# Chunked attention ahead of an expert router: the attention of a tile spread over six iterations, row sums taken from a ones column

## The chip, the cores and the metric

The kernel runs on one core of a Trainium2 chip. The metric is the device time of one execution in microseconds (us). Engines are named as in the profile: PE is TensorE, with PEld its weight loads; DVE is VectorE; ACT is ScalarE; POOL is GpSimd; SP is SyncE, here only a queue that issues DMA transfers.

## What is computed

Two blocks follow each other. The first is attention inside chunks of 64 rows, the second a router that sends each row to one of eight experts.

```
q, k, v: (B=8, H=8, S=576, Dh=64), fp32;  N = B*S = 4608, D = H*Dh = 512
for each batch, head and chunk of 64 rows:
    scores = (q k^T) / 8;  a = exp(scores - rowmax);  a /= rowsum(a) + 1e-9
    out = a v
x = out as (4608, 512)
logits = (x/|x|) (emb/|emb|)^T / tau            # 8 experts
expert = argmax(logits);  gate = softmax(logits)[expert]
y = gate * (relu(x w1[expert]) w2[expert])      # w1 (8,512,1024), w2 (8,1024,512)
```

## The kernel before

The order of instructions on every engine is the order in which the program text issues them; each engine works through its own queue in that order and waits on semaphores where data or a buffer is not ready.

**Attention.** The 4608 rows are 36 tiles of 128 rows; a tile holds two chunks of each of eight heads, which are four pairs. `load_qk` fetches a q and a k tile (256 KB each, in pieces of 256 bytes, split in two where a tile straddles two batches) through SP's queue; `load_v` fetches a whole batch of v as eight transfers, one for each head. For a tile t:

- `turn_qk` transposes k and q on PE (four 128x128 transposes each) and copies kT by ACT and qT by DVE from PSUM to SBUF.
- `scores` makes 16 products of 64x64 (each shows as two instructions in the profile), takes the row maximum and subtracts it on DVE, applies exp on ACT, and sums the rows on DVE (the line `nc.vector.tensor_reduce(rs, a, ...)`), adds 1e-9 and inverts.
- `turn_a` transposes the weights a and copies aT by ACT.
- `values` makes 16 products with v, multiplies by the inverted sums on DVE into x, writes x to DRAM through POOL's queue, and squares x on ACT with a running sum into `nsq`.
- `turn_x` transposes x and copies xT by DVE; `logits` multiplies it with the normalised expert embeddings into one PSUM bank that holds the logits of all tiles.

One iteration t of the loop issues, in this order: `turn_a(t)`, `turn_qk(t+1)`, `scores(t+1)`, `turn_x(t-1)`, `values(t)`, the loads for later tiles, and `logits(t-1)`. The output of `values` goes into the other half of the PSUM banks that held the tile's scores. Every fourth iteration `load_first` fetches one of eight 2 MB weight matrices (w1 and w2 of expert 0 and expert 7, and each a second time into the second slots).

[...] Before, the pool `ps_s` has two tiles of two banks, `ps_t` (all transposes) three of one, `ps_l` one.

**Seam.** A chain of small DVE operations and 36 products sorts the rows by expert into 40 blocks.

**Experts.** For each of the 40 blocks rows are gathered, transposed, multiplied by w1, passed through relu, transposed, multiplied by w2, scaled and scattered. The weights lie in two slots on each of two sides; a block whose expert's weights are not yet in its slot loads them.

The functions around the change:

## Time and profile before

| | |
|---|---|
| median of 3 runs | 1045.79 us (1044.2 to 1046.27) |
| profiled execution, its own time | 1047.4 us |
| span of the profiled execution | 1045.6 us |
| PE busy in the span | 907.6 us (87%) |
| DVE busy | 268.5 us (26%) |
| ACT busy | 173.1 us (17%) |
| POOL busy | 103.9 us (10%) |
[...]

Times in the rows are microseconds from the span's start. Busy time is the time in which an engine has an instruction in work. Matmuls overlap each other, so the distance between two starts says more than a duration. [...]

### The profile page before, as it was taken

To read this page: it belongs to the slowest core of one execution; us is meant where nothing else is said; L and a number is where in the kernel's file an instruction comes from. 1 tells how busy PE (TensorE), PEld (TensorE's weight loads), DVE (VectorE), ACT (ScalarE), POOL (GpSimd) and SP (SyncE) were. 2 spreads that over 40 slices of the span, in tenths; PEclk is the share of its full clock that TensorE was granted. 3 is DMA by queue.
4 is the path that set the end of the run, shared out by engine and by line. 5 is a ranking of instruction groups with operands and counts; after the bars stand their busy time and mean duration, and the time that the engine had idled before them with its cause. 6 is when DMAs were issued, how large, how long until landed. Compare 5 with 4: busy or idle time off the path is not lost.

```text
span 1045.6 us, 15287 instructions
## 1 busy us (share of the span) xinstructions
PE 907.6 (87%) x6287; PEld 485.3 (46%) x6287; DVE 268.5 (26%) x508; ACT 173.1 (17%) x310; POOL 103.9 (10%) x128
## 2 busy tenths in 40 slices
PE   4777777767777745899999999999999999999998
PEld 4666666656666635333333333333333333333332
DVE  3444444343444466111111111111111111111110
ACT  3222222222222220011111011011111101101111
POOL 0000000000000000101111101101110110111101
PEclk9855555555555555899999999999999999999999
DMA  8555465457374100101013575167942142316670
GB/s 204 147 150 168 113 185 171 116 162 200 88 207 133 40 21 1 51 19 41 21 41 121 202 261 202 41 226 285 345 162 106 51 186 106 121 41 233 229 256 2
DMA packets 153670, 142.58 MB, mean 136 GB/s; under 512 B 115702, under 2 KB 115702, under 8 KB 153600
## 3 DMA queue, kind: packets, MB, share of 16 engines
q1 hardware_dynamic: 144256, 112.21, 34.6%
q0 software_dynamic: 9344, 29.39, 7.9%
q8 instruction: 50, 0.82, 0.3%
q14 instruction: 20, 0.16, 0.0%
HBM read 391.14 MB, written 19.92 MB: 393 GB/s over the span
## 4 chain that ended last, share of the span: by engine, by line
issue 56%; PE 21%; DVE 14%; POOL 5%; ACT 2%; POOLq 0%; DMA 0%; SPq 0%
PE lg_ps L226 6%; PE tr L136 6%; PE sc L154 4%; POOL xin L515 4%; PE tr L181 3%; DVE mx L162 2%; DVE a L164 2%; DVE qT L141 2%; DVE rs L172 2%; ACT a L170 2%; DVE xT L220 2%; POOL out_dram L583 2%; PE inv L451 1%; DVE rs L173 1%; DMA kx<-in_k_dram 0%
## 5 line engine op out<-in xcount | busy, mean ns | idle before, releaser
L541 PE MATMUL h_ps<-w,xbT 128*64 128x512 f32 x1280 | 284.5, 597 | 2.4 <-DVE xbT L531 2.4
L574 PE MATMUL y_ps<-w,hT 128*64 128x512 f32 x1280 | 283.3, 595 | 0.0
L541 PEld LDWEIGHTS h_ps<-w,xbT 128*64 128x64 f32 x1280 | 92.3, 138 | 186.5 <-issue 183.3
L574 PEld LDWEIGHTS y_ps<-w,hT 128*64 128x64 f32 x1280 | 88.5, 137 | 167.0 <-issue 167.0
L552 DVE TENSOR_SCALAR h<-h_ps 128x512 f32<-128x512 f32 x40 | 27.7, 692 | 377.9 <-PE h_ps L541 377.9
L226 PE MATMUL lg_ps<-enT,xT 128*128 128x8 f32 x288 | 64.2, 352 | 62.3 <-DVE xT L220 62.3
L583 POOL DMA_INDIRECT out_dram<-y,dst_row x40 | 40.6, 1014 | 532.6 <-ACT y L582 517.2
L226 PEld LDWEIGHTS lg_ps<-enT,xT 128*128 128x128 f32 x288 | 60.8, 312 | 69.2 <-DVE xT L220 69.1
L582 ACT ACTIVATE y<-y_ps,gate_at 128x512 f32<-128x512 f32 x40 | 27.5, 688 | 272.9 <-PE y_ps L574 272.9
L550 ACT ACTIVATE h<-h_ps 128x512 f32<-128x512 f32 x40 | 23.9, 598 | 285.1 <-PE h_ps L541 285.1
L154 PE MATMUL sc<-kT,qT 64*64 64x64 f32 x1152 | 40.7, 317 | 31.5 <-DVE qT L141 31.5
L566 DVE COPY hT<-ht_ps 128x512 f32<-128x512 f32 x40 | 27.7, 692 | 136.6 <-PE ht_ps L562 136.6
L141 DVE COPY qT<-tr 128x512 f32<-128x512 f32 x36 | 24.9, 691 | 136.5 <-PE tr L136 136.5
L154 PEld LDWEIGHTS sc<-kT,qT 64*64 64x64 f32 x1152 | 35.0, 218 | 44.9 <-issue 42.4
L209 POOL DMA_DIRECT2D x_rows<-x x36 | 19.6, 544 | 352.3 <-DVE x L202 352.3
L562 PEld LDWEIGHTS ht_ps<-ident,h 128*128 128x128 f32 x320 | 34.3, 140 | 32.5 <-issue 32.5
L515 POOL DMA_INDIRECT xin<-x_rows,src_row x40 | 41.0, 1024 | 49.5 <-DVE dst_row L465 37.6
L170 ACT ACTIVATE a<-a 128x512 f32<-128x512 f32 x36 | 22.7, 630 | 132.5 <-DVE a L164 132.5
L562 PE MATMUL ht_ps<-ident,h 128*128 128x128 f32 x320 | 43.7, 280 | 0.0
L194 PE MATMUL sc<-v,aT 64*64 64x64 f32 x1152 | 40.8, 318 | 0.0
L136 PE MATMUL tr<-ident,kx 128*128 128x128 f32 x144 | 36.4, 405 | 4.9 <-DMA kx<-in_k_dram 4.9
L218 PE MATMUL tr<-ident,x 128*128 128x128 f32 x144 | 40.0, 433 | 0.0
(118 smaller groups left out, 605.4 us busy)
## 6 DMA issues: line engine op xcount, KB each, us to landing
w<-in_moe_w_dram SPq DMA_DIRECT2D x168, 2048.0 KB
v<-in_v_dram SPq DMA_DIRECT2D x64, 144.0 KB
x_rows<-x POOLq DMA_DIRECT2D x36, 256.0 KB, 2.3
qx<-in_q_dram SPq DMA_DIRECT2D x32, 256.0 KB
kx<-in_k_dram SPq DMA_DIRECT2D x32, 256.0 KB
qx<-in_q_dram SPq DMA_DIRECT2D x8, 128.0 KB
kx<-in_k_dram SPq DMA_DIRECT2D x8, 128.0 KB
xin<-x_rows,src_row POOLq DMA_INDIRECT x40, 3.5
```

Source lines behind the costliest of these rows:

```text
L136: nc.tensor.transpose(ps[:, i], a[:, i * P : i * P + P], ident)
L141: nc.vector.tensor_copy(x, ps)
L154: nc.tensor.matmul(sc[CH * c : CH * c + CH, par, i], lhsT=qx[r0 : r0 + CH, i, c0 : c0 + CH], rhs=kx[r0 : r0 + CH, i, c0 : c0 + CH], start= ...
L170: nc.scalar.activation(a, a, AF.Exp, scale=scale)
L194: nc.tensor.matmul(pv[CH * c : CH * c + CH, par, i], lhsT=d["aT"][r0 : r0 + CH, i, CH * c : CH * c + CH], rhs=v_t[b][r0 : r0 + CH, i, cb], ...
L218: nc.tensor.transpose(ps[:, c], d["x"][:, c * P : c * P + P], ident)
L226: nc.tensor.matmul(lg_ps[:, t], lhsT=d["xT"][:, c], rhs=enT[:, c], start=(c == 0), stop=(c == KD - 1),)
L515: nc.gpsimd.indirect_dma_start(out=t, out_offset=None, in_=x_rows, in_offset=bass.IndirectOffsetOnAxis(ap=src_row[:, j : j + 1], axis=0), ...
L541: nc.tensor.matmul(ps[G * s : G * s + G], lhsT=d["xT"][:, c, G * s : G * s + G], rhs=w1_sb[s][j % 2][:, c, fh * 512 : fh * 512 + 512], sta ...
L562: nc.tensor.transpose(ps[:, c], d["h"][:, f0 : f0 + P], ident)
L574: nc.tensor.matmul(ps[G * s : G * s + G], lhsT=d["hT"][:, c, G * s : G * s + G], rhs=w2_sb[s][j % 2][:, c], start=(c == 0), stop=(c == KF ...
L583: ins = nc.gpsimd.indirect_dma_start(out=out, out_offset=bass.IndirectOffsetOnAxis(ap=dst_row[:, j : j + 1], axis=0), in_=y, in_offset=Non ...
```

## The change

An iteration t now issues: `turn_a(t)`, `turn_qk(t+3)` with the load of tile t+7 behind it, `logits(t-2)`, `scores(t+2)`, `turn_x(t-1)`, `values(t)` with loads of v, `weights(t+2)` (the exp alone), `norm(t)` (the square alone). The loop runs from -3 to 37. Each v tile has a column of ones behind the 64 columns of a head (in rows of 72), filled by POOL, so that the products of `values` have 65 columns, the last of which is the row sum; the sum on DVE is gone, and 1e-9 and the inversion follow the products. The products of `values` have two PSUM banks of their own, and the scores' pool has one tile of two banks instead of two such tiles. xT is copied by ACT instead of DVE. Of the eight weight loads four are issued together in iteration 12; the other four, for the second slots, are issued behind the attention's part, in a pool that is opened there.

```diff
-    w1_sb = [[keep.tile([P, KD, F], FP32, name=f"w1_{s}{i}") for i in range(2)] for s in range(2)]
+    w1_sb = [[keep.tile([P, KD, F], FP32, name=f"w1_{s}0")] for s in range(2)]
...
+    def load_first(i):
+        for s in range(2):
+            e = (0, E - 1)[s]
+            nc.sync.dma_start(out=w1_sb[s][i], in_=w1_rows[:, e * KD : e * KD + KD, :])
...
+    VW = 72
-        tc.tile_pool(name="qk", bufs=3) as qk_p,
+        tc.tile_pool(name="qk", bufs=4) as qk_p,
-        tc.tile_pool(name="ps_s", bufs=2, space=PSUM) as ps_s,
+        tc.tile_pool(name="ps_s", bufs=1, space=PSUM) as ps_s,
+        tc.tile_pool(name="ps_v", bufs=1, space=PSUM) as ps_v,
...
-            t = v_p.tile([P, NPAIR, NCB, Dh], FP32, tag="v", name="v")
+            t = v_p.tile([P, NPAIR, NCB, VW], FP32, tag="v", name="v")
+            nc.gpsimd.memset(t[:, :, :, Dh : Dh + 1], 1.0)
             for h in range(H):
                 r0 = CH * (h % 2)
                 nc.sync.dma_start(
-                    out=t[r0 : r0 + CH, h // 2],
+                    out=t[r0 : r0 + CH, h // 2, :, 0:Dh],
...
-            a = wk.tile([P, NPAIR, 2, CH], FP32, tag="a", name="a")
+            a = wk.tile([P, NPAIR, 2, CH], FP32, tag="a", name="a", bufs=3)
...
+            st[t] = {"a": a}
+
+        def weights(t):
+            a = st[t]["a"]
             nc.scalar.activation(a, a, AF.Exp, scale=scale)
-            rs = wk.tile([P, NPAIR, 2], FP32, tag="rs", name="rs")
-            nc.vector.tensor_reduce(rs, a, axis=AX.X, op=ALU.add)
-            nc.vector.tensor_scalar(rs, rs, 1e-9, None, ALU.add)
-            nc.vector.reciprocal(rs, rs)
-            st[t] = {"ps": ps, "a": a, "rs": rs}
...
-            pv = d["ps"][:, :, NPAIR * CH :].rearrange("p r (i d) -> p r i d", d=Dh)
+            ps = ps_v.tile([P, 2, 512], FP32, tag="pv", name="pv")
+            pv = ps[:, :, 0 : NPAIR * (Dh + 1)].rearrange("p r (i d) -> p r i d", d=Dh + 1)
...
-                            rhs=v_t[b][r0 : r0 + CH, i, cb],
+                            rhs=v_t[b][r0 : r0 + CH, i, cb, 0 : Dh + 1],
...
+            rs = wk.tile([P, 2, NPAIR], FP32, tag="rs", name="rs")
+            nc.vector.tensor_scalar(rs, pv[:, :, :, Dh], 1e-9, None, ALU.add)
+            nc.vector.reciprocal(rs, rs)
+            x = wk.tile([P, NPAIR, 2, Dh], FP32, tag="x", name="x", bufs=3)
             nc.vector.tensor_tensor(
                 x.rearrange("p i r d -> p r i d"),
-                pv,
-                d["rs"].rearrange("p i r -> p r i").unsqueeze(3).to_broadcast([P, 2, NPAIR, Dh]),
+                pv[:, :, :, 0:Dh],
+                rs.unsqueeze(3).to_broadcast([P, 2, NPAIR, Dh]),
...
+        def norm(t):
             junk = one.tile([P, D], FP32, tag="junk", name="junk")
-            nc.scalar.activation(junk, x, AF.Square, accum_out=nsq[:, t : t + 1])
+            nc.scalar.activation(junk, st[t]["x"], AF.Square, accum_out=nsq[:, t : t + 1])
...
-            nc.vector.tensor_copy(xT, ps)
+            nc.scalar.copy(xT, ps)
...
-        for t in range(NT + 1):
+        for t in range(-3, NT + 2):
+            if 0 <= t < NT:
                 turn_a(t)
-            if t + 1 < NT:
-                turn_qk(t + 1)
-                scores(t + 1)
-            if t > 0:
+            if t + 3 < NT:
+                turn_qk(t + 3)
+                if t + 7 < NT:
+                    load_qk(t + 7)
+            if 0 <= t - 2:
+                logits(t - 2)
+            if 0 <= t + 2 < NT:
+                scores(t + 2)
+            if 0 <= t - 1 < NT:
                 turn_x(t - 1)
-            if t < NT:
+            if 0 <= t < NT:
                 values(t)
-                if t + 4 < NT:
-                    load_qk(t + 4)
                 b = (2 * t + 2) // NCB + 1
                 if b not in v_t and b < B:
                     load_v(b)
-                if t % 4 == 3 and t // 4 < 8:
-                    load_first(t // 4)
-            if t > 0:
-                logits(t - 1)
+                if t == NT // 3:
+                    load_first(0)
+            if 0 <= t + 2 < NT:
+                weights(t + 2)
+            if 0 <= t < NT:
+                norm(t)
+            if t == -2:
+                set_up_experts()
...
+    late_p = ctx.enter_context(tc.tile_pool(name="late", bufs=1))
+    for s in range(2):
+        w1_sb[s].append(late_p.tile([P, KD, F], FP32, name=f"w1_{s}1"))
+        w2_sb[s].append(late_p.tile([P, KF, D], FP32, name=f"w2_{s}1"))
+    load_first(1)
```

Ahead of the loop the loads are now q and k of tiles 0 and 1, the first batch of v, tiles 2 and 3, and the second batch of v.

## Rows read from the trace of the kernel before

**Rows 1.** By stage: busy PE, PEld, DVE, ACT, POOL; clock, DMA share, GB/s.

```profile
21.60:378.60 357.00, 264.86 (x3052) 229.63 (x3052) 149.54 (x280) 87.29 (x176) 19.59 (x36) 0.54 0.50 141
378.60:420.70 42.10, 16.32 (x75) 15.68 (x75) 29.60 (x95) 3.24 (x4) 3.77 (x7) 0.50 0.04 8
420.70:1045.60 624.90, 618.00 (x3040) 232.70 (x3040) 83.02 (x120) 74.91 (x120) 78.56 (x78) 0.99 0.39 140
```

**Rows 2.** The page: granted clock of TensorE in 40 slices, tenths.

```profile
PEclk9855555555555555899999999999999999999999
```

**Rows 3.** Timeline of one iteration: start, duration, engine, line, operation, [idle before <- releaser].

```profile
190.15 1.11 PE L218 MATMUL tr<-ident,x 128*128 128x128 f32 x4
...
191.19 1.13 PE L194 MATMUL sc<-v,aT 64*64 64x64 f32 x32
...
192.40 0.69 DVE L172 TENSOR_REDUCE rs<-a 128x8 f32<-128x512 f32 x1 [0.70 <-ACT a L170]
193.12 0.17 DVE L173 TENSOR_SCALAR rs<-rs 128x8 f32<-128x8 f32 x1
193.32 0.20 DVE L174 RECIPROCAL rs<-rs 128x8 f32<-128x8 f32 x1
193.44 0.64 DVE L220 COPY xT<-tr 128x512 f32<-128x512 f32 x1
194.00 0.68 DVE L202 TENSOR_TENSOR x<-sc,rs 128x512 f32<-128x512 f32 x1
...
194.14 1.87 PE L226 MATMUL lg_ps<-enT,xT 128*128 128x8 f32 x8 [1.81 <-DVE xT L220]
194.77 0.63 ACT L211 ACTIVATE junk<-x 128x512 f32<-128x512 f32 x1 [2.41 <-DVE x L202]
...
195.86 1.09 PE L181 MATMUL tr<-ident,a 128*128 128x128 f32 x4
...
196.75 1.06 PE L136 MATMUL tr<-ident,kx 128*128 128x128 f32 x4
197.00 0.59 ACT L183 COPY aT<-tr 128x512 f32<-128x512 f32 x1 [1.50 <-PE tr L181]
...
197.60 1.06 PE L136 MATMUL tr<-ident,qx 128*128 128x128 f32 x4
...
199.54 1.13 PE L154 MATMUL sc<-kT,qT 64*64 64x64 f32 x32 [0.87 <-DVE qT L141]
...
200.60 0.69 PE L218 MATMUL tr<-ident,x 128*128 128x128 f32 x2
```

**Rows 4.** The same columns for four stretches around one rise of the clock.

```profile
122.66:127.20 4.54, 4.53 (x20) 4.13 (x20) 0.55 (x1) 1.89 (x4) 0.54 (x1) 0.50 0.15 58
128.20:131.30 3.10, 3.10 (x68) 2.47 (x68) 1.38 (x2) 0.58 (x1) 0.00 (x0) 0.50 1.03 225
131.60:134.90 3.30, 1.78 (x16) 1.78 (x17) 1.99 (x5) 0.92 (x3) 0.54 (x1) 1.00 1.00 398
135.20:138.40 3.20, 2.32 (x39) 1.84 (x38) 1.07 (x2) 0.58 (x2) 0.00 (x0) 0.50 0.82 274
```

**Rows 5.** Timeline of PE in a stretch at the full clock.

```profile
40.86 1.06 PE L226 MATMUL lg_ps<-enT,xT 128*128 128x8 f32 x8 [1.81 <-DVE xT L220]
...
41.77 0.63 PE L181 MATMUL tr<-ident,a 128*128 128x128 f32 x4
...
42.24 0.60 PE L136 MATMUL tr<-ident,kx 128*128 128x128 f32 x4
...
42.68 0.92 PE L136 MATMUL tr<-ident,qx 128*128 128x128 f32 x4
```

**Rows 6.** The same columns: a full queue; weights; x; a stretch of v.

```profile
2.00:21.00 19.00, 8.40 (x120) 7.28 (x120) 6.29 (x14) 5.82 (x11) 0.81 (x2) 1.00 1.05 239
50.00:53.00 3.00, 3.00 (x16) 3.00 (x17) 0.06 (x1) 1.31 (x3) 0.54 (x1) 0.50 1.01 406
32.00:33.00 1.00, 1.00 (x6) 1.00 (x6) 0.00 (x0) 0.00 (x0) 0.00 (x0) 1.00 0.66 254
192.40:198.40 6.00, 4.26 (x20) 4.13 (x20) 2.21 (x5) 1.86 (x4) 0.54 (x1) 0.50 0.75 188
```

## The prediction

> **What bounds the kernel now.** I read the busy time by stage first, then the page's clock row, then one iteration of the attention loop in order of time, with its waits, on the matmul engine (PE), VectorE (DVE) and ScalarE (ACT), and at last stretches for the clock and the transfers. The program has three stages [rows 1]: attention until 378.6 us, a seam of 42.1 us that plans the experts' blocks, and the experts' part of 624.9 us, in which PE is busy 618 us at the full clock. The change touches the first. There PE is busy 264.9 of 357 us at a granted clock of 0.54, DVE 149.5, ACT 87.3 and the DMA engines half the time: nobody is full. The reader should see in the page's clock row the digit 5 over nearly this whole stage [rows 2].

> One iteration takes 10.45 us, from one transposition of x to the next, 190.15 to 200.60 [rows 3]. Its seven groups on PE, by the distance to the next start, less the waits: x transposes (TX) 1.04, values (V) 1.13, logits (LG) 1.72, weights' transposes (TA) 0.89, k 0.85, q 1.07, scores (SC) 1.06: 7.76 us of work. The other 2.68 us are two waits, 1.81 for xT before the logits and 0.87 for qT before the scores [rows 3]. In each, DVE has only just made what PE wants. [...]

> **The order of work.** Afterwards, what an iteration's PE group reads was made an iteration earlier, except aT, which has five groups between its transposes and V. Both waits of PE, 2.68 us, lose their cause. With no wait, q's last transpose overlaps the next group like k's, 0.86 instead of 1.07, so the slow pace is 7.55 us. V takes 65 columns for 64, 0.02 us.

> DVE loses the row sums (0.69) and xT (0.64) and keeps x at 0.68, qT, max and subtraction, which move as much and are priced at 0.69 each like the row sums, and the two small ones of 0.17 and 0.20 [rows 3]: 3.1 us an iteration. ACT gains xT; I price it as its aT copy, 0.59, and with kT of the same shape, the square at 0.63 and exp priced like it, it has 3.0 us. Neither is a bound at 7.55 us, nor quite at 4.

> Where do the stalls go? The tightest loop left: V, sum and reciprocal and x on DVE (0.17, 0.20 and 0.68), the square on ACT (0.63), behind it in ACT's queue the aT copy (0.59), which frees the transposes' buffer (three buffers, four tiles an iteration) for TX, then V. With TX and V that is 2.27 us and four hand-overs of 0.09, as between x's end and the square's start [rows 3], 0.4, plus 1.04 + 1.13 at the slow level: 4.8 us; 3.6 to 4.2 at the fast one. It is under 7.55 and about at PE's own pace when fast. The single score buffer makes SC wait for max and subtraction of the tile before, 1.4 us, while 6.5 us of other groups lie between at the slow clock, and half of that at a doubled one. POOL gets eight small fills; it is busy 19.6 us in 357 [rows 1].

> **The clock** decides the size. In this stage it rises four times, one of them in [rows 4], each time when SC, TX and V have run without a gap: busy 3.10 of 3.10 us, then 1.00 for the next 3.3 us, in which PE works 1.78 us, then 0.50 again. Before it lie 4.54 us of logits and transposes, as gapless, and the clock stayed [rows 4]. (The 1.00 printed ahead of 39 us is no record: transposes take 1.06 there as later.) After the change SC, TX, V, TA, K and Q follow each other, 5.8 us without a gap at the slow level, in every iteration; I take it that the clock rises within the first iterations that have all their data. Fast prices [rows 5]: LG 0.91, TA 0.47, k 0.44; q and TX like k, 0.45. SC and V are in no fast row; they lie between half (0.53) and no gain (1.06). The rows at hand halve, but none of them has instructions this short, so I take the middle, 0.8. Sum 2.72 + 1.6 = 4.3 us, bounds 3.8 and 4.85. Whether the clock stays is the open point: after PE is busy 54% of a stretch it fell [rows 4]; in the experts' part, near 99%, it held [rows 1]. The loop would be over 90% busy by the same count, so I take it as held.

> LG and three groups of transposes did not raise the clock; SC, TX and V, a third of it transposes, did [rows 4]. [...]

> **Transfers.** They were hidden; at 4.3 us they are not. q, k and v moved 239 GB/s while the queue was full, 2 to 21 us, and 188 in a stretch of v alone; weights 406 [rows 6]. A q and k tile (0.524 MB) is 2.2 us; a batch of v (1.18 MB, eight issues) 4.9 us at the one rate and 6.3 at the other, 5.7 between them, 8 in 36 iterations, 1.27; writing x took 0.66 us of all engines. Together 4.12 us an iteration, just under PE. The loads run four tiles ahead, each when the transposes of its buffer are through; behind a waiting load, SP's queue holds the v loads and weights, all in order, and PE's transposes wait for them.

> Start: iteration 1 transposes tile 4, loaded behind four tiles and two batches: 5 x 0.524 + 2 x 1.18 = 4.98 MB at 239 GB/s from 2.0 us, 23 us. The first weights: instead of one 2 MB load every fourth iteration, four are issued together at iteration 12, 8.4 MB at 406, 20.7 us, ahead of the next tiles in the same queue. PE then runs dry; the lead by then is 11 x (4.3 - 4.12) = 2 us, leaving 18.7. The other four move to behind the stage: 20.7 us in a seam of 42 us where DMA is busy 4% [rows 1], needed only by the experts' second block. I cost them at nothing; without that cover, 20.7 us.

> **Sum.** 23 to iteration 1; 35 x 4.3 = 150.5; 2 for the last xT and logits; 18.7 for the weights; 6.5 for two stretches at the slow level, at the start and after the dry time (one iteration each, 7.55 for 4.3). The stage ends at 200.7. A check by transfers alone: 23 + 31 x 2.2 + 6 x 5.7 + 34 x 0.66 + 20.7 = 169, then four iterations and the end, 19: no sooner than 188. Against 378.6 the gain is 177.9; 1047.4 - 177.9 = 869.5 for a profiled execution, which stood 1.6 above the median of the runs: 868 us. With PE at 3.8 the transfers set the end, 186, 853; with 4.85, where they hide behind PE and the lead covers 8 of the weights' 20.7, 23 + 170 + 2 + 12.7 + 6.5 = 214, 881.

> **Rivals.**
> Clock goes up and down (27%). It falls again after each fast stretch, as in all rows of this stage. A fast stretch of 3.3 us does 5.8 slow us of work; with 3.4 to 10.5 slow us between, the pace is 5.5 to 6.4, say 6.0. For it: the clock never held here [rows 4]. Against: those fast stretches were half idle. 23 + 210 + 2 + 3 = 238, a time of 905 (890 to 918).
> Transfers bind harder (8%). If all of q, k and v go at the 188 GB/s of v's stretch: 23.3 MB after the start 124 us, with x 22 and weights 21, on a start of 28: 195, and 19 more, 214: 881. For it: the DMA share was already 1.05 in the full stretch.
> Clock stays slow (10%). 23 + 35 x 7.55 + 2 = 289, gain 89, 956. For it: 4.54 gapless us that left the clock low.
> The queues tie the iterations (3%), the other side. If aT's copy, stuck behind the square, and the single buffers for scores and values let no tile overlap the next, a tile is one chain: q 1.06, qT 0.69, SC 1.06, max and subtraction 1.4, exp 0.63, TA 1.09, aT 0.59, V 1.13, sum to x 1.05, TX 1.11, xT 0.59, LG 1.9: 12.3 us. 25 + 35 x 12.3 = 455: 1122. It decides from a pace of (378.6 - 25)/35 = 10.1 us. Against it stand the 3.6 to 4.8 us worked out above.
> No effect (2%): the gain of the loop is given back, which would need 178 us elsewhere; the late weights alone can take 21.

> **How the numbers follow.** The forecast's case, fast and near the transfers, has 50%, with a range of its own of 850 to 885. The range takes it, the harder transfers and most of the up and down: 846 to 925, with the 7 us at the low end for transfers above 239 GB/s. A difference under 0.2% (2 us) can't be told from none. Slower holds 3%, same 2%, faster 95%.

> **What would show it.** In the changed profile: the stage's last logits near 200 us; PE waits for qT and xT gone; the clock row at 9 over most of the first fifth but for a hole near 70 to 95 us, where PE waits for DMA; a DMA row of 8 to 9. Right only in part: PE dense and the clock at 5 (third rival) or between (first); SC or V over 1 us at the full clock. The prediction is wrong if PE waits every iteration on ACT's or DVE's copy at a pace over 5 us, or if the experts' part no longer takes 625 us.

## The result, and the profile after

The changed kernel takes 864.3 us (median of 4 runs) against 1045.0 for the kernel before: a ratio of 0.827, interval 0.8245 to 0.8294. The forecast was 868. The profiled execution has a span of 860.2 us, 185.4 less than before. In two experiments below one run of four was clearly longer than the others, 921.9 us in the old order and 1035.1 us with the ones column alone; their ratios go by the other three.

The page's rows for the granted clock and the DMA engines, in 40 slices of 21.5 us. The granted clock is a share of full speed: in these traces 1.00 in the fast stretches and 0.50 in the slow ones [rows 4], with means between where a stretch holds both (0.86 from 26 to 27 us of the changed kernel, whose scores slow down at 26.7).

```profile
PEclk9999789995589999999999999999999999999999
DMA  9999999929110001045763157875214252147560
```

Where [rows 2] had a run of fives, the clock is now high but for a hole in the fifth and sixth slice (86 to 129 us, digits 7 and 8; the two fives behind are the seam) and the start, where the first digit does not fit the durations (four transposes of q, k or a take 1.06 to 1.12 us until 19 us, 0.60 to 0.66 in the loop), and DMA is full until the stage is nearly over. By stage, with the columns of [rows 1] (start of the steady part, seam, experts), and then two stretches inside the first:

```profile
25.30:194.20 168.90, 149.01 (x3000) 134.16 (x3000) 102.21 (x203) 98.69 (x205) 20.02 (x41) 0.92 0.94 246
194.20:236.60 42.40, 16.32 (x75) 15.67 (x75) 29.61 (x95) 3.24 (x4) 3.72 (x7) 0.50 0.54 205
236.60:860.20 623.60, 616.68 (x3040) 232.40 (x3040) 83.01 (x120) 74.96 (x120) 78.63 (x78) 1.00 0.39 140
92.70:107.40 14.70, 0.22 (x3) 0.01 (x1) 0.94 (x3) 1.82 (x4) 0.54 (x1) 0.58 1.03 365
107.40:115.50 8.10, 7.91 (x88) 6.56 (x88) 3.06 (x6) 1.73 (x3) 0.00 (x0) 0.50 1.07 209
```

Attention ends at 194.2 instead of 378.6 us. The seam and the experts' part kept their lengths, with the 8.4 MB of the four late weight loads now inside the seam (its DMA share went from 0.04 to 0.54). So 184.4 of the 185.4 us are gained in the stage that the change touches. One iteration on PE, to hold against [rows 3]:

```profile
34.07 0.66 PE L178 MATMUL tr<-ident,a 128*128 128x128 f32 x4
34.57 0.60 PE L136 MATMUL tr<-ident,kx 128*128 128x128 f32 x4
35.00 0.60 PE L136 MATMUL tr<-ident,qx 128*128 128x128 f32 x4
35.44 0.96 PE L229 MATMUL lg_ps<-enT,xT 128*128 128x8 f32 x8
36.33 0.69 PE L152 MATMUL sc<-kxT,qxT 64*64 64x64 f32 x32
36.95 0.65 PE L221 MATMUL tr<-ident,x 128*128 128x128 f32 x4
37.54 0.69 PE L192 MATMUL pv<-v,aT 64*64 64x65 f32 x32
38.16 0.55 PE L178 MATMUL tr<-ident,a 128*128 128x128 f32 x3
```

From 34.07 to 38.16 is 4.09 us where it was 10.45; this time of one iteration is called the pace below. No row has a bracket: PE waits for nothing. Scores and values, which had no fast row before, take 0.62 us each to the next start. What PE waits for between 20 and 200 us (total, times, longest), the three largest rows:

```profile
PE tr L136 <- DMA kx<-in_k_dram: 18.3, 4, 14.5
PE pv L192 <- ACT aT L180: 1.3, 3, 0.6
PE tr L136 <- ACT junk L215: 0.9, 1, 0.9
```

The waits for qT and xT are gone from the loop; the one large wait is for a k tile, 14.5 us in one piece. Its cause stands in the order of time:

```profile
77.51 2.01 SPq L77 DMA_DIRECT2D w<-in_moe_w_dram  x2
...
79.57 11.18 SPq L80 DMA_DIRECT2D w<-in_moe_w_dram  x2
...
90.85 4.26 SPq L112 DMA_DIRECT2D kx<-in_k_dram  x1
...
92.26 0.66 PE L178 MATMUL tr<-ident,a 128*128 128x128 f32 x4
...
107.42 1.08 PE L136 MATMUL tr<-ident,kx 128*128 128x128 f32 x4 [14.50 <-DMA kx<-in_k_dram]
```

The four weight loads of iteration 12 hold SP's queue for 13 us; the next k load is issued at 90.85, PE has used up its tiles at 92.7 and comes back at 107.4, at the slow level (1.08 us for four transposes) for another 8 us.

### The profile page after: what moved, and what is told of

It is laid out like the page before. It is cut to its first block, busy times and chain, and to the rows that moved or that the text cites. A ratio compares the mean times of both kernels' runs of the same rounds, so it can differ in the third digit from the quotient of the medians.

```text
span 860.2 us, 15300 instructions
## 1 busy us (share of the span) xinstructions
PE 794.9 (92%) x6287; PEld 392.8 (46%) x6287; DVE 223.8 (26%) x436; ACT 187.4 (22%) x346; POOL 105.2 (12%) x136
## 4 chain that ended last, share of the span: by engine, by line
issue 69%; PE 15%; POOL 7%; DMA 4%; DVE 3%; POOLq 0%; ACT 0%; SPq 0%; DVEq 0%; ACTq 0%
POOL xin L530 5%; PE tr L136 3%; PE lg_ps L229 2%; PE sc L152 2%; DMA kx<-in_k_dram 2%; POOL out_dram L598 2%; PE inv L466 2%; PE pv L192 2%; PE tr L178 2%; PE tr L221 2%; DMA qx<-in_q_dram 2%; POOL x_rows L210 1%; DMA x_rows<-x 0%; SPq L112 0%; POOLq L530 0%
## 5 line engine op out<-in xcount | busy, mean ns | idle before, releaser
L136 PE MATMUL tr<-ident,kx 128*128 128x128 f32 x144 | 24.1, 294 | 22.3 <-DMA kx<-in_k_dram 22.3
L210 POOL DMA_DIRECT2D x_rows<-x x36 | 19.6, 544 | 168.7 <-DVE x L203 140.3
L229 PEld LDWEIGHTS lg_ps<-enT,xT 128*128 128x128 f32 x288 | 35.9, 196 | 1.0 <-ACT xT L223 0.9
L229 PE MATMUL lg_ps<-enT,xT 128*128 128x8 f32 x288 | 35.5, 250 | 0.7 <-ACT xT L223 0.7
L141 DVE COPY qxT<-tr 128x512 f32<-128x512 f32 x36 | 24.9, 692 | 36.1 <-PE tr L136 34.3
L160 DVE TENSOR_REDUCE mx<-sc 128x8 f32<-128x512 f32 x36 | 24.9, 692 | 26.9 <-PE sc L152 26.9
L546 DVE COPY xbT<-x_ps 128x512 f32<-128x512 f32 x40 | 27.7, 692 | 13.8 <-PE x_ps L544 9.3
L544 PE MATMUL x_ps<-ident,xin 128*128 128x128 f32 x160 | 24.5, 277 | 5.2 <-DMA xin<-x_rows,src_row 5.2
L466 PE MATMUL inv<-rr,oh 128*128 128x80 f32 x72 | 15.7, 422 | 14.6 <-DVE oh L465 14.6
L136 PEld LDWEIGHTS tr<-ident,kx 128*128 128x128 f32 x144 | 18.1, 151 | 23.7 <-issue 15.2
```

What stands on the lines that cost most here:

```text
L136: nc.tensor.transpose(ps[:, i], a[:, i * P : i * P + P], ident)
L210: nc.gpsimd.dma_start(out=x_rows[P * t : P * t + P, :], in_=x)
L229: nc.tensor.matmul(lg_ps[:, t], lhsT=d["xT"][:, c], rhs=enT[:, c], start=(c == 0), stop=(c == KD - 1),)
L466: nc.tensor.matmul(inv.rearrange("p t k -> p (t k)"), lhsT=oh, rhs=rr[:, s].rearrange("p t k -> p (t k)"), start=(s == 0), stop=(s == NT - 1),
L546: nc.vector.tensor_copy(xT, ps)
```

## Experiments

Theory at the start: the spread order takes both waits away, PE runs gapless, the clock goes up and stays; transfers and the weights' burst take some back. Rivals: the ones column and xT on ACT are the gain, not the order; the clock alone; transfers.

**Late weights.** The four loads leave iteration 12.

```diff
-                if t == NT // 3:
+                if t == NT - 8:
                     load_first(0)
```

> The changed kernel, but the four weight loads of iteration 12 are issued in iteration 28, behind the last q and k load. Theory: the dry time of PE near 93 to 107 us (14.5 us) and the 8 us at the lower clock behind it come from these loads standing ahead of q and k in one queue, so both vanish: the stage ends near 176 instead of 194 us, the time is 18 us less (846), with no hole in the clock row. Rival: the transfers as a whole set the stage's end (169 plus the last iterations by the prediction's check), so that moving 8.4 MB within the stage only moves the wait: under 5 us less.

849.0 us, ratio to the kernel before 0.8121 (0.8087 to 0.8156): 15 us less than the changed kernel. The dry time and the hole in the clock row are gone, and from 60 to 140 us PE is busy all the time with a DMA share of 1.05:

```profile
PEclk8999999865699999999999999999999999999999
60.00:140.00 80.00, 80.00 (x1743) 73.36 (x1742) 58.98 (x117) 57.04 (x119) 11.43 (x25) 1.00 1.05 249
```

So it was the place in the queue and not the bytes of the stage. The attention ended at 175.9 as expected, 18 us sooner; 3.7 of them went in the seam, which took 46.1 us for 42.4, as the loads now ran beside x's last writes, for which the seam's first DVE operation waits:

```profile
179.80 0.17 DVE L314 MEMSET onesb<- 128x128 bf16 x1 [3.45 <-DMA x_rows<-x]
```

**Old order with the other parts.** The loop of the kernel before around the ones column, the own banks and xT on ACT, with the loads ahead of the loop back in the old order too (shown in short).

```diff
-        for t in range(-3, NT + 2):
+        for t in range(NT + 1):
             turn_a(t)
-            turn_qk(t + 3); logits(t - 2); scores(t + 2); turn_x(t - 1)
-            values(t); weights(t + 2); norm(t)
+            turn_qk(t + 1); scores(t + 1); turn_x(t - 1)
+            weights(t + 1); values(t); norm(t); logits(t - 1)
```

> The changed kernel's parts (ones column, two PSUM banks for the values, xT copied by ACT) in the old order: q and k of tile t+1, its scores, x of tile t-1, values of t, logits of t-1 in one iteration. Theory: the spread over iterations is what takes the waits away and keeps PE gapless; here the wait for xT goes (the row sums left DVE) but 0.87 us for qT stays, the clock stays mostly low, the pace is 8.6 us and the time near 980. Rival: the ones column and xT on ACT, which shorten DVE's chain, are the gain, and the order is not needed: 865 to 900.

894.0 us, 0.8541 (0.8524 to 0.8558). The theory's 980 fell and the time lies in the rival's range: five sixths of the gain is there without the spread order. The page's clock row and a piece of the loop on PE:

```profile
PEclk9999979999558999999999999999999999999999
59.82 0.69 PE L152 MATMUL sc<-kxT,qxT 64*64 64x64 f32 x32 [0.88 <-DVE qxT L141]
60.45 0.66 PE L221 MATMUL tr<-ident,x 128*128 128x128 f32 x4
61.03 0.70 PE L192 MATMUL pv<-v,aT 64*64 64x65 f32 x32
61.78 1.06 PE L229 MATMUL lg_ps<-enT,xT 128*128 128x8 f32 x8
...
65.19 0.52 PE L152 MATMUL sc<-kxT,qxT 64*64 64x64 f32 x20 [0.88 <-DVE qxT L141]
```

The wait before the logits is gone, the one for qT is there in every iteration (0.88 us), the pace is 5.37 us, and still the clock holds, but for 107 to 121 us, around a wait of 8.3 us for a k tile. What the order adds is 1.28 us of pace: 0.88 is that wait, and 0.40 lies in the groups around it, which start closer together in the spread order (V to logits 0.75 us here, V to the next group 0.62 there). That is 43.5 us in 34 iterations, while the two kernels are 29.7 us apart: the old order lost less to the weights (8.3 us of dry PE instead of 14.5), and the rest was not taken apart. That 34 x 0.88 is 29.9 too is chance.

**The clock alone.** Fillers on PE in the waits of the kernel before (shown in short; `lg_ps` is also made wider for them).

```diff
+        def fill(n):
+            for _ in range(n):
+                nc.tensor.matmul(lg_ps[:, NT : NT + 16], lhsT=ident, rhs=ident, start=True, stop=True)
...
                 turn_qk(t + 1)
+                fill(3)
                 scores(t + 1)
...
                     load_first(t // 4)
+                fill(10)
             if t > 0:
```

> The kernel before, with filler products of the identity with itself (128x128, into unused columns of the logits' bank) behind the values (10) and between q's transposes and the scores (3); all waits of the data stay. Theory: PE is busy without a gap, so the clock goes to its full level and stays; the loop is then the old chain with PE's groups on it halved, 10.45 less 2.55 = 7.9 us, the time near 958. With the gain of the waits alone at the slow clock (about 90 us, 956) that makes up the whole change. Rival 1: the clock does not follow from gapless work (or falls again each iteration): the fillers lengthen the slow loop by 3 us, and the time is above 1100. Rival 2: the clock alone is nearly all of the gain: under 900.

967.4 us, 0.925 (0.9234 to 0.9265). From 20 to 300 us the clock never falls:

```profile
PEclk9999999999997579999999999999999999999999
152.17 0.69 PE L160 MATMUL sc<-kT,qT 64*64 64x64 f32 x32 [0.20 <-DVE qT L141]
...
154.01 2.50 PE L148 MATMUL lg_ps<-ident 128*128 128x128 f32 x20
156.78 1.06 PE L232 MATMUL lg_ps<-enT,xT 128*128 128x8 f32 x8 [0.27 <-DVE xT L226]
...
160.07 0.89 PE L160 MATMUL sc<-kT,qT 64*64 64x64 f32 x32 [0.20 <-DVE qT L141]
```

The pace is 7.90 us, as worked out. More work on PE made the kernel 78 us faster, with every wait of the data kept. (The 958 was 9 too low: it took 2.55 us off every iteration of 10.45, but with its four short fast spells the kernel before needed 10.1 on average, and 35 x 2.2 is 77.) Both rivals are out.

**Row sums on DVE again.** The changed kernel without the ones column, with v's rows 64 wide again (shown in short).

```diff
+            nc.vector.tensor_reduce(rs, a, axis=AX.X, op=ALU.add)      # in weights(t), behind the exp
-            nc.gpsimd.memset(t[:, :, :, Dh : Dh + 1], 1.0)
```

> The changed kernel without the ones column: the row sums are taken by DVE behind the exp, at the end of the iteration, then 1e-9 and the inversion, as before. Theory: DVE goes from about 3.1 to 3.8 us in an iteration of 4.1, so the ones column is worth little: 0 to 8 us more than the changed kernel. Rival: the reduction waits on the exp in DVE's in-order queue and holds the qT copy and the max of the next iteration, which closes a loop through ACT: a pace of 4.8 or more, over 890.

862.0 us, 0.8247 (0.8222 to 0.8272): not to be told from the changed kernel, and the rival is out. DVE is busy 17.6 of 20 us in the steady part (60 to 80 us) and PE 20 of 20. In the spread order with xT on ACT the ones column is worth nothing that these runs can show.

**One line: xT by ACT.** In the kernel before.

```diff
-            nc.vector.tensor_copy(xT, ps)
+            nc.scalar.copy(xT, ps)
```

> The kernel before with one line changed: xT is copied by ACT. After the run with the old order the theory is: what held PE back was DVE's queue, in which xT stood behind row sums that wait for the exp; taking xT or the sums off DVE lets PE run almost gapless in the old order too, and the rest is the clock. Here xT still follows the exp in ACT's queue: the wait before the logits falls from 1.81 to about 0.7 us at the slow level (pace 9.35), 1.6 at the fast one (pace 6.6 with 0.88 for qT). If the clock holds at 62% busy: 252 us for the stage, near 920. If it goes up and down: 940 to 1000. Rival (the waits alone count, the clock does not move): 34 x 1.1 = 37 us less, 1008.

950.0 us, 0.9081 (0.9064 to 0.9097). The case of a clock that goes up and down:

```profile
PEclk9979779797785599999999999999999999999999
106.96 0.69 PE L154 MATMUL sc<-kT,qT 64*64 64x64 f32 x32 [0.88 <-DVE qT L141]
...
110.31 1.06 PE L226 MATMUL lg_ps<-enT,xT 128*128 128x8 f32 x8 [1.45 <-ACT xT L220]
...
113.61 0.69 PE L154 MATMUL sc<-kT,qT 64*64 64x64 f32 x32 [0.88 <-DVE qT L141]
```

Waits of 2.33 us in a fast iteration of 6.65; the clock rises, stays for some iterations and falls. One line gives 96 us, over half of the change's gain, and the rival's 1008 is out.

**Ones column alone,** with its banks; xT stays on DVE. The code is that of the changed kernel's `load_v` and `values` in the kernel before, with v's rows 65 wide instead of 72; as in the changed kernel, the scores' pool has one tile.

> The kernel before with the ones column and the values' own banks, nothing else: xT stays on DVE but no longer behind the row sums. Theory: slow pace 8.6 as only qT's 0.87 is left, fast pace 5.9 (xT is done 2.2 us behind the scores, the values 1.25), 70% busy: the clock rises and mostly holds, the time is 905 to 930. Rival (only the spread order or ACT frees PE): above 985.

950.4 us, 0.9052 (0.9009 to 0.9095): slower than the 905 to 930 expected.

```profile
PEclk9998866777585599999999999999999999999999
101.03 0.69 PE L156 MATMUL sc<-kT,qT 64*64 64x64 f32 x32 [0.88 <-DVE qT L143]
...
103.93 1.06 PE L228 MATMUL lg_ps<-enT,xT 128*128 128x8 f32 x8 [0.98 <-DVE xT L222]
...
107.22 0.69 PE L156 MATMUL sc<-kT,qT 64*64 64x64 f32 x32 [0.88 <-DVE qT L143]
```

The fast pace, 6.19 us, is near the 5.9 forecast, but with 1.86 us of waits in it the clock does not hold. That was the miss. At the slow level only qT's wait is left, 0.87 us in 8.73, and the clock still stays low from 112 to 135 us. The rival (only order or ACT frees PE) is out too.

**xT on DVE** in the changed kernel.

```diff
-            nc.scalar.copy(xT, ps)
+            nc.vector.tensor_copy(xT, ps)
```

> The changed kernel with xT copied by DVE as before. Theory: in the spread order the copies have slack, DVE has 3.75 us of a 4.1 us pace: 0 to 4 us more than the changed kernel (864 to 868). Rival: DVE, in order, makes qT or the max late in each iteration and the pace goes to 4.6: 882.

869.2 us, 0.8298 (0.8273 to 0.8324). The intervals overlap, so by the times it costs a few us at most. The trace does show a cost in the loop, a pace of 4.28 us for 4.09:

```profile
41.66 0.69 PE L152 MATMUL sc<-kxT,qxT 64*64 64x64 f32 x32
...
45.94 0.69 PE L152 MATMUL sc<-kxT,qxT 64*64 64x64 f32 x32
```

The rival's 4.6 is excluded.

**All weights behind the attention, v later.** (Shown in short.)

```diff
-        load_v(1)                          # ahead of the loop
+            if t == -2: load_v(1)          # behind the load of tile 5
-                if t == NT // 3:
-                    load_first(0)
+    load_first(1); load_first(0)           # behind the attention
```

> The changed kernel with all eight weight loads behind the attention's part (second slots first) and the second batch of v issued behind tile 5 instead of ahead of tile 4. Theory: in the run with the late weights the dry time went, but their 20.7 us held up the last writes of x and with them the seam by 3.6 us; behind the attention they cost nothing (41 us in a seam of 42), and the later v lets PE start about 4 us sooner: 838 to 843. Rival: the first block then waits for its weights, and the seam grows by 10 us or more: over 850.

844.6 us, 0.8075 (0.8054 to 0.8096), a little over the expected range and under the rival's 850. PE reaches tile 4 at 21.0 us instead of 25.3, as expected, but then waits 1.5 us for a k tile at 29.2; the stage ends at 174.3, only 1.6 us before that of the late weights. And PE now waits 7.9 us for the first gathered rows instead of 5.2. This trace also shows, at its very start, the clock's rise among transposes alone:

```profile
3.83 1.09 PE L136 MATMUL tr<-ident,kx 128*128 128x128 f32 x4 [3.83 <-DMA kx<-in_k_dram]
4.83 1.12 PE L136 MATMUL tr<-ident,qx 128*128 128x128 f32 x4
5.74 1.07 PE L136 MATMUL tr<-ident,kx 128*128 128x128 f32 x4
6.96 0.63 PE L136 MATMUL tr<-ident,qx 128*128 128x128 f32 x4
```

The changed kernel's own start, with the same four groups from 3.94 us on, has no such rise:

```profile
7.29 1.09 PE L136 MATMUL tr<-ident,qx 128*128 128x128 f32 x4 [0.17 <-DMA qx<-in_q_dram]
8.31 1.13 PE L152 MATMUL sc<-kxT,qxT 64*64 64x64 f32 x32
```

**Two of the eight in iteration 28.** The version above, with w1 of the first slots issued there and the rest behind the attention.

> The version with all weights behind the attention, but w1 of the first slots (two of eight loads, 10 us) goes in iteration 28 behind the last q and k load, and the rest behind the attention as w1 second, w2 first, w2 second slots. Theory: with all eight behind, 41 us of weights still run when the first rows are gathered, and that gather came 2.6 us later (7.9 us of PE waiting for it instead of 5.3); with 31 us left the gather meets an empty queue: 841 to 843. Rival: the 10 us hold up x's last writes as all four loads did (seam 3.6 us longer): 846 or more.

841.9 us, 0.8054 (0.8036 to 0.8072), the fastest version that computes the whole task, 22 us under the changed kernel. Its step over the version above is within the intervals; what it was made for is in the waits of PE from 200 to 222 us (above first, then this one):

```profile
PE x_ps L543 <- DMA xin<-x_rows,src_row: 7.9, 1, 7.9
```

```profile
PE x_ps L549 <- DMA xin<-x_rows,src_row: 5.3, 1, 5.3
```

**Without q's loads.** The expectation names the version with all weights behind the attention; the edit was made on the one after it, with two of the eight in iteration 28, and 841.9 us is what to compare with.

> The version with all weights behind the attention, with q's loads left out: the scores are made from k's tile in place of q, so the scores and what follows are other numbers. A third of the q, k and v bytes is gone. Theory: PE's own 4.09 us is the pace, and transfers set only the start (PE reaches tile 4 some 10 us sooner) and the short waits: the stage ends near 160 instead of 174 us, the time is near 831, the pace stays at 4.1. Rival: the transfers, full until 140 us, set the pace and slow PE's own reads too; then the pace falls under 4.0 and the stage ends before 150: under 822.

835.5 us, 0.7987 (0.7973 to 0.8). The pace is 4.09 us still:

```profile
60.23 0.66 PE L225 MATMUL tr<-ident,x 128*128 128x128 f32 x4
...
64.32 0.66 PE L225 MATMUL tr<-ident,x 128*128 128x128 f32 x4
```

With a third of the q, k and v bytes gone PE's pace does not move: transfers set part of the start and the short waits, not the loop. They are worth some 6 us (the stage ends at 167.3 for 173.1, the time is 6.4 less), under what was expected (160 and 831). The miss is the start: PE reaches tile 4 at 21.5 us for 23.0 and not 10 us sooner, as the start has a wait of 5.3 us for the expert embeddings, the same with q's loads as without.

## Why the prediction was right

*What bounds the kernel, and the clock.* Right for waits for copies on a PE at its slow level (a granted clock of 0.54 in the stage [rows 1]): fillers alone raise the clock and give 78 us with all waits kept; the pace falls from 10.45 to 7.90 and, with the waits gone, to 4.09. The other side, the waits gone at the slow level, was not run. That it stays up, the open point, came out as taken: no fall in a steady stretch of the changed kernel; it fell where PE waited for data (92.7 to 107.4 us) and twice for some 3 us after shorter waits: at 26.7 us (waits of 2.91 and 0.26) and at 136.1 us (0.30 and 0.87).

*Transposes and the clock.* In the run with all weights behind the attention, three groups of four transposes and nothing else ran from 3.83 to 6.8 us at about 1.1 us each, and the fourth took 0.63 us. The run with xT on DVE has the same rise (0.66 us for the fourth group, at 7.26 us). It does not come every time: in the changed kernel's own start sixteen transposes (1.09 to 1.12 us for four) and the scores behind them (1.13 us) stayed slow. The third rival rested on the 4.54 gapless us that left the clock low [rows 4]; why it stayed low there is open.

*Where the stalls go.* Right for the spread order: no loop through ACT shows in the steady part. What the prediction did not see is that its parts replace each other. The wait for xT, 1.81 us, came from DVE's queue, where xT stood behind row sums that wait for the exp (0.70 us [rows 3]); the ones column takes all of it away at the slow level and leaves 0.98 us at the fast one, xT on ACT leaves 0.56 and 1.45, and the two together take it away at the fast level too. The spread order does so with either one of them; without both it was not run. The sum was right because it was made for all parts together; "both waits lose their cause" by the order is true of that order, yet only the wait for qT was shown to need it, which with what hangs on it is 1.28 us of pace and some 30 us in all.

*The terms.* Start 23: iteration 1's transposes at 25.3. Pace 4.3: 4.09, as SC and V came out at 0.62 instead of 0.8 each, while TX took 0.59 for 0.45 (35 x 0.21 = 7 us). For the 32 of SC that is 19 ns from one start to the next; the middle between half and no gain was the author's estimate. Dry time 18.7: 14.5, and at 92.7 us, not 70: the lead was four tiles already issued ahead of the weights, and the loss is a queue delay of 13 us of issue and 16 of transfer less that lead, not a burst less a slack of 2 us; that 18.7 came near it is in part luck. Slow stretches 6.5: 8.1 us at the slow level cost about 3.8 and two shorter ones 1.6 each, 7. End 200.7: 194.2. Pace and dry time erred to the same side, start to the other, and some 2 us of waits under 1 us each were in no term. The profiled execution took 862.0 us where 869.5 was forecast; that the medians, 864.3 and 868, lie closer is chance of the runs.

*The rivals.* Up and down did not happen here, but it is real: it is what the two single parts do (950 us). Harder transfers: 245 to 249 GB/s in the full stretches against 239 at the start [rows 6], and the run without q, with the same pace of 4.09 us, shows that they do not set it. Tied queues and no effect: excluded by the pace.

*The late weights.* Priced at nothing: right for the four of the changed kernel, whose seam is 42.4 us long against 42.1. The price appears when they meet something: 14.5 us of dry PE behind four in iteration 12, 3.7 us when they met x's last writes, 2.7 when they met the first gather.

## What to carry to other kernels

Before breaking a chain up over iterations, look which instruction stands ahead of the late one in its engine's queue: one copy moved to another engine gave 96 of 181 us. In this kernel waits on PE were paid twice, as time and as clock: with 2.68 us of waits gone an iteration went from 10.45 to 4.09 us, 6.36 less, and the single parts, which left 2.33 and 1.86 us of them in a fast iteration, stopped at 950 us. A large prefetch is judged by what it stands ahead of in its queue: the same 8 MB cost 15 us more in the middle of the loop than near its end, and 3 us or less behind it.
